# Query and key preparation re-timed, and a bias row copied by another engine, in a fused attention and gated-MLP kernel

## The chip, the core and the metric

The kernel runs on one core of a Trainium2 chip. The core has five engines that run side by side, each in the order of its own instruction list: TensorE (PE, matrix products), VectorE (DVE), ScalarE (ACT), GpSimd (POOL) and SyncE (SP, here only a queue that issues transfers). Transfers run on 16 DMA engines. The metric is the device time of one execution in microseconds (us). The kernel before has a median of 343.76 us over 13 runs (342.1 to 346.02).

## The reference

Attention with normalised queries and keys is followed by a gated MLP with a spatial mix over the sequence. There are 8 batches, 12 heads, a sequence of 448 and a head size of 64; the model width is 768 and the hidden width 1024.

```python
def rmsnorm(x, g):
    rms = np.sqrt(np.mean(x * x, axis=-1, keepdims=True) + 1e-06)
    return x / rms * g
q_n, k_n = (rmsnorm(q, g_q), rmsnorm(k, g_k))
scores = scale * np.matmul(q_n, k_n.transpose(0, 1, 3, 2))
scores = scores - np.max(scores, axis=-1, keepdims=True)
attn = np.exp(scores)
attn = attn / (np.sum(attn, axis=-1, keepdims=True) + 1e-09)
attn_out = np.matmul(attn, v)
# x: attn_out with the heads of a token side by side, (8, 448, 768)
h = np.maximum(x @ w_in, 0.0)
u, v = (h[..., :d_ff // 2].copy(), h[..., d_ff // 2:].copy())
v_n = (v - mu) / np.sqrt(var + 1e-06)
v_s = np.einsum('ts,bsd->btd', w_spatial, v_n) + b_spatial[None, :, None]
gated = u * v_s
return gated @ w_out
```

## The kernel before

**Groups and steps.** Four heads of one batch form a group G; there are 24 groups, three to a batch (b = G // 3). The keys of two heads at a time are split into 7 chunks, so all the work on scores is 168 passes p (group p // 7, chunk p % 7). Two passes make a step s, so a group takes three and a half steps. Passes 0 to 19 are done one at a time in the early part (`early(p)`); steps 10 to 83 form the main loop. In each step TensorE computes scores (line 367, and line 363 for the mixed chunk), ScalarE takes their exponential (`expo`, line 374), and the rest of TensorE's time is filled from a list of MLP pieces (`work`, `fill`), except in a step in which a group is finished (`attend`: weights times v, line 396, with the reciprocal on ScalarE, lines 403 and 404, and the product on VectorE, line 411). The order is written out by hand: the program's order of calls is each engine's order of instructions. After step 83 only the rest of the last batch's MLP remains.

**Preparing q and k.** Before a group's scores can start, six things are done for q (i = 0) and k (i = 1): loading; `squares` on GpSimd (line 250; a few on ScalarE, line 248); `reduce` on VectorE (line 258); `rstd` on ScalarE (lines 266 and 267, for q and k at once); `scaled` (line 277, on GpSimd except for a few early ones); a transpose. The first four groups are transposed by TensorE, all others by a DMA transpose that SP issues (`transpose_dma`, line 341); q is then ready as qT, while k lands as kr and VectorE multiplies it by the combined gains (`k_scale`, line 347, writing kT). The main loop takes these actions out of `todo`, which holds for each step what is to be done for which group. EVEN and ODD give the steps as offsets from 7 * (G // 2), the step in which an even group's scores begin; an odd one's begin in the middle of the step at offset 3. `at` puts a transpose one step after its `scaled`.

**Loads.** Groups 1 to 5 are loaded one by one (`load`, four DMAs for q and four for k, three rotating buffers each). From batch 2 on, q and k of a whole batch are loaded in four parts each (`load_part`, line 105), into two buffers that alternate by batch; the second buffer exists from step 17, when the early buffers are given up. `load_v` loads and converts v of a batch in four parts, issued on GpSimd's queue (line 130), into one of two tiles, also alternating. The weights come over GpSimd's queue as well: `load_w_in` (line 199, one half of w_in each), `load_w_sp` (lines 204 and 205) and `load_w_out` (line 209).

**The spatial weights.** In the MLP of batch 0, after the matmuls of u, `bias_row` writes the spatial bias into a row of the transposed spatial weights w_spT, and `w_sp_unit` transposes w_spatial on TensorE (line 218) and copies it out on VectorE (line 223). bias_row is three VectorE copies of one partition:

```python
dve.tensor_copy(out=main[:, :, 0:64],
                in_=b[:, 0:256].rearrange("o (r m) -> o m r", m=4)[:, 0:3, :])
dve.tensor_copy(out=main[:, :, 64:128], in_=b[:, 256:S].rearrange("o (r m) -> o m r", m=3))
dve.tensor_copy(out=row[:, 384:S], in_=b[:, 3:256:4])
```

Of the kernel before, what the change touches and what calls it, by code (L numbers as in the profile page):

```python
# [10 lines left out]
FP = mybir.dt.float32  # L11
BF = mybir.dt.bfloat16
AF = mybir.ActivationFunctionType
# [6 lines left out]
def kernel(  # L20
# [76 lines left out]
    def load_part(b, i, part):  # L97
        if part == 0:
            t = qb_pools[b % 2].tile([P, 2 * NG, NCH, D], FP, name="kb" if i else "qb")
            qbs[b, i] = t  # L100
            for g in range(NG):
                raw[NG * b + g, i] = t.rearrange("p (h g) c d -> p h g c d", g=NG)[:, :, g]
        lo, hi = lo_hi((q, k)[i][b])
        tv = qbs[b, i].rearrange("p h c d -> p h (c d)")
        sync.dma_start(
            out=(tv[0:64, :, 0:256], tv[64:128, :, 0:192], tv[64:128, :, 192:448], tv[0:64, :, 256:448])[part],
            in_=(lo[:, 0:6], hi[:, 0:6], lo[:, 6:12], hi[:, 6:12])[part])
# [30 lines left out]
    load_first(1, 1, sync)  # L138
# [12 lines left out]
    load(1, 1, pool)  # L151
# [73 lines left out]
    def bias_row():  # L225
        row = w_spT[64:65, NT - 1, :]
        b = bst[64:65, :]
        main = row[:, 0:384].rearrange("o (m r) -> o m r", r=P)
        dve.tensor_copy(out=main[:, :, 0:64],
                        in_=b[:, 0:256].rearrange("o (r m) -> o m r", m=4)[:, 0:3, :])  # L230
        dve.tensor_copy(out=main[:, :, 64:128], in_=b[:, 256:S].rearrange("o (r m) -> o m r", m=3))
        dve.tensor_copy(out=row[:, 384:S], in_=b[:, 3:256:4])
# [353 lines left out]
    squares(0, 1, 0)  # L586
    reduce(0, 0, 0)
# [23 lines left out]
    def early(p):  # L611
        if p == 0:
            squares(1, 0, eng=act)
            squares(1, 1)
            load_v(0, range(4))
            transpose_first(0, 1, dve)
            transpose_first(1, 1, dve)
        elif p == 2:
            reduce(1, 0)
            reduce(1, 1)  # L620
        elif p == 3:
            rstd(1)
            scaled(1, 0, eng=dve)
            scaled(1, 1, eng=dve)
            squares(2, 0)
            squares(2, 1)
            load_w_in(1)
        elif p == 7:
            reduce(2, 0)
            reduce(2, 1)  # L630
        elif p == 8:
            rstd(2)
            scaled(2, 1)
            scaled(2, 0, eng=dve)
            squares(3, 0)
            squares(3, 1)
            load_w_in(0)
        elif p in (9, 10, 11):
            attend(0, (p - 10,))
        elif p == 14:  # L640
            reduce(3, 0)
            reduce(3, 1)
        elif p == 15:
            rstd(3)
            scaled(3, 1)
            scaled(3, 0, eng=dve)
            squares(4, 0)
            squares(4, 1)
            load_w_sp()
        elif p in (16, 17, 18):  # L650
            attend(1, (p - 17,))
        if p not in (0, 6, 9, 10, 11, 13, 16, 17, 18):
            dummies(6)

    pass_scores(0)
    for p in range(2 * S0):
        expo(psp[p], p, 1)
        if p in (6, 13):
            transpose_pe(p // NCH + 1, 0, dve)
            transpose_pe(p // NCH + 1, 1, dve)  # L660
        if p in (4, 5):
            load(4, p - 4)
        if p in (10, 11):
            load(5, p - 10)
        if p + 1 < 2 * S0:
            pass_scores(p + 1)
        early(p)
# [3 lines left out]
    EVEN = {-8: ("sq", 0), -7: ("sq", 1), -6: ("red",), -5: ("rstd",), -4: ("sc", 0), -3: ("sc", 1), -1: ("ks",)}  # L671
    ODD = {-6: ("sq", 0), -5: ("sq", 1), -4: ("red",), -3: ("rstd",), -2: ("sc", 0), -1: ("sc", 1), 2: ("ks",)}
    todo = {}

    def at(s, G, *what):
        todo.setdefault(s, []).append((G,) + what)
        if what[0] == "sc":
            at(s + 1, G, "tr", what[1])

    at(10, 4, "red")  # L680
    at(11, 4, "rstd")
    at(11, 4, "sc", 0)
    at(11, 4, "sc", 1)
    at(13, 4, "ks")
    at(11, 5, "sq", 0)
    at(12, 5, "sq", 1)
    at(13, 5, "red")
    at(14, 5, "rstd")
    at(14, 5, "sc", 0)
    at(14, 5, "sc", 1)  # L690
    at(16, 5, "ks")
    for G in range(6, NGT):
        for o, what in (ODD if G % 2 else EVEN).items():
            at(7 * (G // 2) + o, G, *what)
    for b in range(2, B):
        s0 = max(S0 if b == 2 else 17, NCH * NG * b // 2 - 17)
        for n in range(8):
            at(s0 + n // (2 if b < 4 else 1), NG * b, "ld", n)

    def prep(s, early_act):  # L700
        for G, what, *i in todo.get(s, ()):
            if (what == "rstd") != early_act:
                continue
            if what == "ld":
                load_part(G // NG, *divmod(i[0], 4))
            elif what == "sq":
                squares(G, i[0])
            elif what == "red":
                reduce(G, 0)
                reduce(G, 1)  # L710
            elif what == "rstd":
                rstd(G)
            elif what == "sc":
                scaled(G, i[0])
            elif what == "tr":
                transpose_dma(G, i[0])
# [7 lines left out]
    v_step = {10 + i: (1, [i]) for i in range(4)}  # L724
# [10 lines left out]
    for s in range(S0, NST):  # L735
        if s == 17:
# [68 lines left out]
```

## Time and profile before

| | value |
|---|---|
| median of 13 runs | 343.76 us (342.1 to 346.02) |
| the profiled execution's own time | 342.37 us |
| its span, first to last instruction | 340.6 us |
| granted TensorE clock, mean | 0.952 |
| step 10 begins its exponential at | 40.80 us |
| step 24 | 105.99 us |
| step 75 | 282.23 us |
| step 83, the last | 309.29 us |
| HBM read and written | 38.55 MB and 11.01 MB |

The profile is one execution. A step is found in it by counting: the exponentials over 128x1792 numbers are those of steps 10, 11, 12 and so on to 83. "Idle before" is the time that an engine stood still ahead of an instruction, with what ended the wait. A busy time of TensorE contains overlap between matmuls that follow each other; what it lost is read from its waits. The share of the DMA engines in a window adds up transfers that overlap, so it can exceed 1.

### The profile page before, as it was taken

The page shows a single profiled execution, that of the slowest core. Times are in us where ns is not written, and L with a number is a line of the kernel's source. Part 1 is how long each engine was busy: PE and PEld are TensorE (multiplying, and loading weights), DVE is VectorE, ACT ScalarE, POOL GpSimd, SP SyncE. Part 2 cuts the span into 40 slices and gives each one's busy share as a digit, 9 for nine tenths or more (in the row PEclk, how much of TensorE's full clock was granted, in tenths as well). Part 3 has the DMA queues.
Part 4 walks back from the last instruction along what each step waited for, and adds up shares of the span by engine and source line. Part 5 has one row for each costly group of instructions (what it writes and reads, how often), then busy time and mean ns, then how long its engine had stood idle before and what let it go on. Part 6 is the DMA issues. An engine that isn't in the chain of part 4 may idle for free.

```text
span 340.6 us, 6451 instructions
## 1 busy us (share of the span) xinstructions
PE 274.7 (81%) x2527; PEld 128.2 (38%) x2537; DVE 212.4 (62%) x343; ACT 211.3 (62%) x273; POOL 205.3 (60%) x183
## 2 busy tenths in 40 slices
PE   6577693690498889788788889779699979999994
PEld 6344330240243344334334344334344433444552
DVE  3885615499939467487467484495397486645652
ACT  2687781392067868567477778658477786675421
POOL 6758893789408499529908698359735993020210
PEclk9799997796589999999999999999799999999998
DMA  6999999939991999936993999857957288131145
GB/s 168 190 213 220 209 176 198 165 48 164 152 163 27 172 185 282 195 64 114 239 213 63 190 190 253 174 102 115 261 120 122 45 172 125 24 93 48 24 139 164
DMA packets 82944, 50.90 MB, mean 149 GB/s; under 512 B 46753, under 2 KB 79170, under 8 KB 82914
## 3 DMA queue, kind: packets, MB, share of 16 engines
q1 hardware_dynamic: 67218, 41.53, 61.7%
q0 software_dynamic: 15408, 8.73, 20.4%
q8 instruction: 20, 0.33, 0.5%
q10 hardware_dynamic: 288, 0.23, 0.2%
q14 instruction: 10, 0.08, 0.1%
HBM read 38.55 MB, written 11.01 MB: 146 GB/s over the span
## 4 chain that ended last, share of the span: by engine, by line
PE 25%; POOL 20%; DMA 18%; DVE 17%; issue 9%; ACT 7%; SPq 4%; POOLq 0%; DVEq 0%; ACTq 0%
DMA kr<-n 9%; POOL sqt L250 8%; POOL n L277 6%; DVE ms L258 6%; PE ps L396 5%; PE ps L527 4%; PE ps L508 4%; ACT et L374 4%; DMA kf<-in_k_dram 4%; PE ps L468 4%; PE ps L498 4%; PE pss L367 3%; DMA vt<-in_v_dram 3%; DVE s L476 3%; POOL vn L490 2%
## 5 line engine op out<-in xcount | busy, mean ns | idle before, releaser
L374 ACT ACTIVATE et<-pss 128x1792 bf16<-128x1792 f32 x74 | 122.8, 1660 | 63.9 <-PE pss L367 53.2
L411 DVE TENSOR_TENSOR xt<-ps,rc 128x448 bf16<-128x448 f32 x48 | 28.1, 620 | 60.0 <-ACT rc L404 47.0
L367 PE MATMUL pss<-qT,kT 64*128 64x448 bf16 x254 | 38.4, 362 | 25.8 <-DVE kT L347 21.4
L250 POOL TENSOR_TENSOR sqt<-kb 128x896 f32<-128x896 f32 x18 | 30.3, 1683 | 46.2 <-DVE ms L258 23.5
L527 PE MATMUL ps<-w_out,gt 128*128 128x384 bf16 (+1 forms) x256 | 47.6, 328 | 3.0 <-DVE osb L445 2.2
L396 PE MATMUL ps<-et,vt 128*32 128x448 bf16 x768 | 44.8, 368 | 5.9 <-DMA vt<-in_v_dram 3.7
L258 DVE TENSOR_REDUCE ms<-sqt 128x14 f32<-128x896 f32 x46 | 47.7, 1075 | 2.6 <-POOL sqt L250 2.6
L468 PE MATMUL ps<-w_in_v,xt 128*128 128x512 bf16 (+1 forms) x182 | 45.4, 381 | 0.4
L498 PE MATMUL ps<-xt,w_in_u 128*128 128x448 bf16 x192 | 40.4, 353 | 2.6 <-DVE osb L445 1.9
L347 DVE TENSOR_SCALAR_CACHE_REDUCE kT<-kr,g_col 128x896 bf16<-128x896 bf16 x20 | 22.7, 1135 | 30.7 <-DMA kr<-n 30.7
L367 PEld LDWEIGHTS <-kT 64*128 64x128 bf16 x276 | 10.5, 94 | 59.8 <-issue 30.5
L527 PEld LDWEIGHTS <-gt 128*128 128x128 bf16 (+1 forms) x256 | 24.2, 100 | 22.6 <-issue 9.3
L396 PEld LDWEIGHTS <-vt 128*32 128x32 bf16 x768 | 22.1, 100 | 24.3 <-issue 11.7
L486 POOL TENSOR_SCALAR nm<-mv 128x4 f32<-128x4 f32 x8 | 1.8, 221 | 48.8 <-DVE mv L477 48.8
L277 POOL TENSOR_TENSOR n<-qb,rs 128x896 bf16<-128x896 f32 x18 | 30.4, 1689 | 0.7 <-ACT rs L267 0.7
L277 POOL TENSOR_TENSOR n<-kb,rs 128x896 bf16<-128x896 f32 x18 | 30.4, 1689 | 0.1
L250 POOL TENSOR_TENSOR sqt<-qb 128x896 f32<-128x896 f32 x18 | 30.3, 1681 | 0.0
L445 DVE COPY osb<-ps 128x384 f32<-128x384 f32 (+1 forms) x45 | 24.4, 556 | 9.3 <-PE ps L527 6.9
L508 PE MATMUL ps<-w_spT,vn 128*128 128x448 bf16 (+1 forms) x128 | 28.7, 369 | 0.0
L490 POOL TENSOR_SCALAR vn<-vs,nm,rv 128x512 bf16<-128x512 bf16 (+1 forms) x32 | 24.0, 764 | 7.1 <-ACT rv L485 6.3
L498 PEld LDWEIGHTS <-w_in_u 128*128 128x128 bf16 x192 | 17.3, 97 | 21.9 <-issue 8.4
L468 PEld LDWEIGHTS <-xt 128*128 128x128 bf16 (+1 forms) x192 | 17.7, 100 | 19.9 <-issue 5.7
(94 smaller groups left out, 363.7 us busy)
## 6 DMA issues: line engine op xcount, KB each, us to landing
out_dram<-osb SPq DMA_DIRECT2D x55, 192.0 KB, 3.8
qb<-in_q_dram SPq DMA_DIRECT2D x12, 384.0 KB, 6.1
kb<-in_k_dram SPq DMA_DIRECT2D x12, 384.0 KB, 6.9
qb<-in_q_dram SPq DMA_DIRECT2D x12, 288.0 KB, 5.5
kb<-in_k_dram SPq DMA_DIRECT2D x12, 288.0 KB, 6.7
vt<-in_v_dram POOLq DMA_DIRECT2D x16, 192.0 KB, 5.2
vt<-in_v_dram POOLq DMA_DIRECT2D x16, 144.0 KB, 5.2
qf<-in_q_dram SPq DMA_DIRECT2D x10, 128.0 KB, 4.1
```

The costliest lines, as they stand in the source:

```text
L250: pool.tensor_tensor(out=t, in0=x, in1=x, op=ALU.mult)
L258: dve.tensor_reduce(out=sqs[gk][:, key[1], :], in_=sqt.pop(key).rearrange("p h c d -> p (h c) d"), axis=AX.X, op=ALU.add)
L277: (eng or pool).tensor_tensor(out=t.rearrange("p c h d -> p h c d"), in0=raw[key], in1=rst[gk][:, key[1], :].rearrange("p (h c) -> p h c", ...
L367: pe.matmul(out=ps[:, h, 0:S], lhsT=kT[r, c0:c0 + 128], rhs=qT[r, :], start=True, stop=True, tile_position=(64 * h, 0))
L374: act.activation(out=ets[s][:, 2 * a:2 * a + 2 * m, :], in_=ps[:, 0:2 * m, 0:S], func=AF.Exp, bias=0.0, scale=1.0)
L396: pe.matmul(out=ps[32 * l:32 * l + 32, 0:S], lhsT=w, rhs=et_of(G, 3 if r == 3 else r + 4 * y, h), start=(r == 0), stop=(r == 3), tile_posi ...
L411: dve.tensor_tensor(out=xts[b][:, 2 * g + half, :], in0=pst.pop((G, half))[:, 0:S], in1=rec[G], op=ALU.mult)
L468: pe.matmul(out=ps[0:m, :], lhsT=xts[b][:, j, t0:t0 + m], rhs=w_in_v[:, j, :], start=(j == 0), stop=(j == 5), tile_position=(0, 0))
L490: pool.tensor_scalar(out=vn_t[b % 2][0:m, c, :], in0=vs[b][c][0:m, :], scalar1=nms[b][0:m, c:c + 1], scalar2=rvs[b][0:m, c:c + 1], op0=ALU ...
L498: pe.matmul(out=ps[:, 0:S], lhsT=w_in_u[:, j, 128 * f:128 * f + 128], rhs=xts[b][:, j, :], start=(j == 0), stop=(j == 5))
L508: pe.matmul(out=ps[:, 0:S], lhsT=vn_t[b % 2][0:kp, c, 128 * f:128 * f + 128], rhs=w_spT[0:kp, c, :], start=(c == 0), stop=(c == NT - 1))
L527: pe.matmul(out=ps[o:o + m, 0:384], lhsT=gts[b][f][:, t0:t0 + m], rhs=w_out[:, f, r], start=(f == 0), stop=(f == 3), tile_position=(0, o))
```

## The change

- `bias_row`: the three copies are made by ScalarE instead of VectorE.
- Start: the second k load of group 0 is issued from ScalarE's queue instead of SP's; the k load of group 1 on GpSimd's queue comes after the first square on that engine; some early squares move between GpSimd and ScalarE; w_in's two halves come earlier on GpSimd's queue.
- v of batch 1 is loaded in pass 9 of the early part, ahead of the spatial weights of pass 15; before, its four parts came in steps 10 to 13.
- Batch 2 (groups 6, 7 and 8) is loaded group by group with `load`. From batch 3 on the whole-batch loads stay, and the second buffer is opened at step 24. They are grouped more tightly: q's four parts in two steps, and k's in two (odd batch) or four (even batch).
- EVEN and ODD become tables that give q and k steps of their own. Squares never fall two in a step in the steady part; `scaled` comes at -6 and -5 (before -4 and -3) for an even group and at -3 and -2 (before -2 and -1) for an odd one. The transposes come at -5 and -4 (before -3 and -2) and at -2 and -1 (before -1 and 0); `k_scale` stays at -1 and 2. Groups 4 to 8 have tables of their own. Inside a step the actions are sorted by ORDER.

```diff
@@ load_part, start
-            t = qb_pools[b % 2].tile([P, 2 * NG, NCH, D], FP, name="kb" if i else "qb")
+            t = qb_pools[(b + 1) % 2].tile([P, 2 * NG, NCH, D], FP, name="kb" if i else "qb")
...
-    load_first(1, 1, sync)
+    load_first(1, 1, act)
...
-    load(1, 1, pool)
@@ bias_row
-        dve.tensor_copy(out=main[:, :, 0:64],
-                        in_=b[:, 0:256].rearrange("o (r m) -> o m r", m=4)[:, 0:3, :])
-        dve.tensor_copy(out=main[:, :, 64:128], in_=b[:, 256:S].rearrange("o (r m) -> o m r", m=3))
-        dve.tensor_copy(out=row[:, 384:S], in_=b[:, 3:256:4])
+        for o, i in ((main[:, :, 0:64], b[:, 0:256].rearrange("o (r m) -> o m r", m=4)[:, 0:3, :]),
+                     (main[:, :, 64:128], b[:, 256:S].rearrange("o (r m) -> o m r", m=3)),
+                     (row[:, 384:S], b[:, 3:256:4])):
+            act.activation(out=o, in_=i, func=AF.Copy, bias=0.0, scale=1.0)
@@ early
     squares(0, 1, 0)
+    load(1, 1, pool)
...
         if p == 0:
-            squares(1, 0, eng=act)
             squares(1, 1)
             load_v(0, range(4))
+            load_w_in(1)
+            squares(2, 1)
+            load_w_in(0)
...
+        elif p == 1:
+            squares(1, 0, eng=act)
...
-            squares(2, 0)
-            squares(2, 1)
-            load_w_in(1)
+        elif p == 4:
+            squares(2, 0, eng=act)
...
-        elif p == 8:
+        elif p == 9:
             rstd(2)
+            scaled(2, 0, eng=dve)
             scaled(2, 1)
-            scaled(2, 0, eng=dve)
             squares(3, 0)
             squares(3, 1)
-            load_w_in(0)
-        elif p in (9, 10, 11):
-            attend(0, (p - 10,))
+            load_v(1, range(4))
...
+        elif p == 19:
+            reduce(4, 0)
+        if p in (10, 11, 12):
+            attend(0, (p - 11,))
...
+        if p in (16, 17):
+            load(6, p - 16)
@@ main loop
-    EVEN = {-8: ("sq", 0), -7: ("sq", 1), -6: ("red",), -5: ("rstd",), -4: ("sc", 0), -3: ("sc", 1), -1: ("ks",)}
-    ODD = {-6: ("sq", 0), -5: ("sq", 1), -4: ("red",), -3: ("rstd",), -2: ("sc", 0), -1: ("sc", 1), 2: ("ks",)}
+    EVEN = {"sq": (-11, -8), "red": (-9, -7), "rstd": (-6,), "sc": (-6, -5), "tr": (-5, -4), "ks": (-1,)}
+    ODD = {"sq": (-9, -7), "red": (-6, -5), "rstd": (-3,), "sc": (-3, -2), "tr": (-2, -1), "ks": (2,)}
+    FIRST = {4: {"red": (None, 10), "rstd": (11,), "sc": (11, 11), "tr": (11, 11), "ks": (13,)},
+             5: {"sq": (10, 11), "red": (11, 12), "rstd": (13,), "sc": (13, 14), "tr": (14, 14), "ks": (16,)},
+             6: {"sq": (13, 14), "red": (14, 15), "rstd": (16,), "sc": (16, 17), "tr": (17, 17), "ks": (20,)},
+             7: {"ldg": (12, 12), "sq": (15, 17), "red": (17, 18), "rstd": (19,), "sc": (19, 19), "tr": (19, 20),
+                 "ks": (23,)},
+             8: {"ldg": (15, 15), "sq": (18, 20)}}
...
-    for b in range(2, B):
-        s0 = max(S0 if b == 2 else 17, NCH * NG * b // 2 - 17)
-        for n in range(8):
-            at(s0 + n // (2 if b < 4 else 1), NG * b, "ld", n)
+    SC8 = 23
+    for b in range(3, B):
+        first_q = max(15 if b == 3 else SC8 + 1, (21 * b - 38) // 2)
+        for n in range(4):
+            todo.setdefault(first_q + n // 2, []).append(("ld", NG * b, n))
+            todo.setdefault(first_q + 2 + (n if b % 2 == 0 else n // 2), []).append(("ld", NG * b, n + 4))
+
+    ORDER = ("red", "rstd", "sc", "sq", "tr", "ks", "ldg", "ld")
...
-    v_step = {10 + i: (1, [i]) for i in range(4)}
+    v_step = {}
...
-        if s == 17:
+        if s == SC8 + 1:
             early_sb.close()
```

## The prediction

> **What bounds the kernel now.** I read the page's busy shares, then TensorE's waits, then the places where its long waits stand. The lines are from the page (three), the waits (four), the timeline around 74 to 90 us (six), the timeline around 160 to 169 us (three) and the windows (three).
>
> ```profile
> PE 274.7 (81%) x2527; PEld 128.2 (38%) x2537; DVE 212.4 (62%) x343; ACT 211.3 (62%) x273; POOL 205.3 (60%) x183
> ...
> PE   6577693690498889788788889779699979999994
> ...
> DMA  6999999939991999936993999857957288131145
> ...
> PE pss L367 <- DVE kT L347: 21.4, 10, 5.0
> PE ps L218 <- DVE w_spT L223: 12.5, 1, 12.5
> PE ps L396 <- DMA vt<-in_v_dram: 3.7, 1, 3.7
> ...
> DVE kT L347 <- DMA kr<-n: 30.7, 9, 7.8
> ...
> 74.11 13.55 DVE L229 CAST w_spT<-bst 1x192 bf16<-1x192 f32 x1
> 74.63 1.68 POOL L277 TENSOR_TENSOR n<-qb,rs 128x896 bf16<-128x896 f32 x1
> ...
> 87.41 1.72 POOL L250 TENSOR_TENSOR sqt<-qb 128x896 f32<-128x896 f32 x1
> 87.58 1.72 DVE L231 CAST w_spT<-bst 1x192 bf16<-1x192 f32 x1
> 89.22 0.19 DVE L232 CAST w_spT<-bst 1x64 bf16<-1x64 f32 x1
> ...
> 89.89 2.05 PE L218 MATMUL ps<-ident,w_sp 128*64 128x128 bf16 x20 [12.54 <-DVE w_spT L223]
> ...
> 161.31 1.31 SPq L341 DMA_TRANSPOSE kr<-n  x1
> ...
> 167.61 1.15 DVE L347 TENSOR_SCALAR_CACHE_REDUCE kT<-kr,g_col 128x896 bf16<-128x896 bf16 x1 [3.80 <-DMA kr<-n]
> ...
> 168.82 0.55 PE L367 MATMUL pss<-qT,kT 64*128 64x448 bf16 x4 [2.47 <-DVE kT L347]
> ...
> 0.00:60.00 60.00, 40.43 (x453) 22.80 (x454) 34.23 (x60) 36.75 (x54) 43.31 (x46) 0.94 1.10 197
> 60.00:110.00 50.00, 33.10 (x279) 14.17 (x282) 39.03 (x44) 24.67 (x33) 31.44 (x26) 0.80 0.88 120
> 110.00:250.00 140.00, 118.93 (x1111) 52.61 (x1115) 85.65 (x146) 96.33 (x118) 96.76 (x81) 0.99 0.94 177
> ```
>
> To be seen: TensorE is the busiest engine, and its strip is at 9 only towards the end; it has a hole at about 77 to 90 us. The second and third wait lines are one event each. The first is ten events, all of one kind: a group's scores stand ready to start, but its kT isn't there. One of the ten, of 5.0 us, is group 4 at 55.98 us; the other nine (16.4 us) lie after 120 us, once in a step that begins a group. The timeline of group 12 shows why: its kr was issued at 161.31, landed 6.3 us later, and VectorE and then TensorE waited for it. The last number of a window line is GB/s, the one before it the share of the DMA engines, the one before that the clock: up to 60 us the transfers run flat out at 197 GB/s; from 60 to 110 us, with the hole in it, only at 120.
>
> The hole has an odd cause. Three bias copies of one partition, 192, 192 and 64 numbers, took 13.55, 1.72 and 0.19 us. Size can't be it, since the first two are equal. From 74.63 to 89.13 us GpSimd ran without a pause, and the copies ended with it.
>
> **What the Trainium skill says.** "SBUF — State Buffer", section "Who interferes with whom": VectorE and GpSimd share a pair of ports under an exclusive lock; a VectorE copy or cast from SBUF to SBUF can enter a two-port mode, and then waits for GpSimd's instruction (or GpSimd for it); "PE and ACT never wait on anyone." The trace agrees so far as the 13.55 us beside a busy GpSimd go. It shows no ScalarE copy of this shape. "DMA: Bandwidth & Descriptors", section "Queues, rings and completion order": each DMA engine takes turns between the queues that have work for it, packet by packet. So a GpSimd load that comes sooner takes time from SP's loads and transposes, and the bytes ahead of a transpose count whichever queue they are in. The trace agrees with this: kr of group 4, issued at 46.70 in the flat-out stretch, landed after 7.9 us, those of quiet stretches after 2.9.
>
> **The change part by part**, against the profiled execution: 342.37 us, of which the span is 340.6.
>
> (a) Bias row on ScalarE. The wait of 12.54 us goes. The clock line helps: it is granted 0.50 at 80 to 90 us and 0.69 at 90 to 100 us, and step 20 takes 3.98 us where neighbours take 3.0; I count 1.0 us for that. Added: three ScalarE instructions. Nearest rows: 0.30 us for 128x4, 0.52 for 128x384; so some 0.35 each, 1.0 in all, in a step in which ScalarE has about half a microsecond idle: 0.5 us on the path. If ScalarE had to wait for the lock as well, the wait would only move; the skill's sentence excludes it, and I take its word. What is late next: steps 20 to 24 need groups 6 and 7. Their kr were issued at 79.1 and 93.9, so with the hole gone the transposes have to come sooner too. Before, VectorE's own list (squares' sums behind the copy) and SP's were held up by the hole; they move with it. Sum: -13.0.
>
> (b) v of batch 1 in pass 9. Before, the last part was issued on GpSimd's queue at 52.61 and landed 10 us later, which held TensorE 3.73 us. Pass 9 comes at about 27 us and its queue there is free of squares by some 31, so v lands by 45, ten microseconds before use: -3.7. Its DMA time isn't new, only earlier.
>
> (c) Group 4's kT (5.00 us). The transposes are issued in step 11 right after the scaling, as before in effect (qT at 44.7, 0.06 us after its scaling). What delays kr is DMA. By SBUF bytes, ahead of it lie groups 0 to 5 (12 x 0.46 MB), batch 2's q (1.38), v of batches 0 (0.69) and 1 (a quarter), w_in (1.57) and w_sp (0.40): 9.7 MB, and 9.7 MB at 197 GB/s is 49 us. After: group 6 alone in place of batch 2's q (0.92), but all of v 1: 9.8 MB. So it is about as late. The gain is between 0 and 5.0; I take 2.0, since nothing of GpSimd's queue competes any more while it travels.
>
> (d) The nine later waits, 16.4 us. Groups 8, 10, 12, 14, 16 and 18 (even) make 12.4 of them, and in each VectorE waited for kr (1.2 to 4.4 us). Their transposes move two steps, about 6 us, sooner at 3.0 us a step: all six should go. Group 13 (0.95, kr landed late) moves one step: goes. Groups 11 and 17 (1.54 and 1.53) had kr landed 10 us before; there VectorE was late with its own list, where the multiplication keeps its place behind the statistics of the MLP: they stay. Together 13.3; but loads are denser (four parts in two steps, up to 1.38 MB in 6 us, 230 GB/s against the 177 of the window) and a kr may fall behind them, so I take -12.0. Bounds: -4 to -16.4.
>
> (e) The early part, up to step 10. The first k square comes before k of group 1 is fetched, so that fetch starts at about 8.4 instead of 2.7 us and its square ends near 16.7; the sums of pass 2 were done after 17 us anyway. The pass gets one more square on ScalarE (0.94 us), which is loaded there: +0.5. GpSimd's queue takes DMA share earlier (w_in's second half at about 23 instead of 31 us), so groups 3 and 4 land later, perhaps 2 us; against it SP's loads start two issues (1.3 us) sooner. Bounds -1.5 to +3; taken +0.5.
>
> (f) Whole-batch loads, and single-group loads for batch 2: 16 more DMAs on SP at 0.6 us, 10 us of SP's time. SP waited 72.6 us for GpSimd's scaling alone, so this costs nothing; without that cover it would delay transposes, which is the first rival.
>
> Sum: -13.0 - 3.7 - 2.0 - 12.0 + 0.5 = -30.2, or 312.2 us for the profiled execution. That one lies 0.4% under the median of 343.76, so the forecast is 313 us. A test against bytes: to begin step 24, at 105.99 before, the loads of batches 0 to 3, w_in, w_sp and the transposes up to group 7, some 17 MB, must be through; at 197 GB/s that is 86 us. My parts (a) to (c) and (e) put step 24 at 88. So there is hardly any room left there, and the DMA engines are the next bound up to step 24.
>
> **Rivals.** *The transfers take over* (0.23): the hole goes, but the DMA engines, flat out up to 90 us and then in denser bursts, bring kr late, so that of (c) nothing and of (d) only 4 us come, and the early part loses 2: 342.4 - 13.0 - 3.7 - 4 + 2 = 323.7, in the median 325. For it: share 1.10 and 0.94. Against: four or five steps of notice for kr where there were two or three. *Everything goes* (0.08): all of (c) and (d) and nothing early: 342.4 - 13.0 - 3.7 - 5 - 16.4 = 304.3, median 305. *The copy isn't cured* (0.03): ScalarE needs as long on single-partition rows; only (b) to (e) come, about 329. Against it: 1.72 us for equal work. *Slower* (0.06): kr behind the bursts. Each of the 19 groups after the fourth has about 9 us (three steps) from kr's issue to its multiplication; median landing is 5.6, the longest seen 12.1. To lose the 17 us of (a) and (b) and the 16.4 that are there now, every group would have to wait 1.8 us, which takes a landing of 11 us in the median, twice the present one: then 344 or more.
>
> **How the numbers follow.** The main case has 0.60, with its own range of 308 to 318. The range for 8 in 10 takes in most of the second case and the third: 304 to 327. Half a per cent, about 1.7 us, is what a measurement of this kernel tells from no change. Faster by more: 0.60 + 0.23 + 0.08 + 0.03 = 0.94; the last case gives 0.01 to no change and 0.05 to slower.
>
> **What would show it.** (a) right: no w_spT wait over 1 us, and the ScalarE copies under 1 us each. (b): no wait of line 396 for v. (c): group 4's wait at 3 us. (d): the wait of scores for kT falls from 21.4 to about 7, with two of 1.5 us left. (e): step 10 between 39 and 44 us. (f) and the first rival: kr landing in the median above 8 us, and VectorE waiting for kr over 20 us. Wrong altogether if step 24 begins after 95 us, or if steps 24 to 75 take more than 172 of their 176.2.

## The result, and the profile after

The changed kernel takes 317.67 us in the median of 11 runs (312.48 to 322.59), against 343.8 us for the kernel before in the runs beside it. The ratio is 0.919, with a 95% interval of 0.9145 to 0.9228: some 8% faster, 26 us between the medians. The ratio compares only the executions within 1.5% of the fastest of each kernel, so it lies a little below 317.67 / 343.8 = 0.924, and the profiled execution after, at 319.19 us, isn't among these while that before is. The forecast of 313 us was 4.7 us too low, and 317.67 lies in its range of 304 to 327. The profiled execution has a span of 317.3 us, 23.3 us shorter than that of the profile before. Line numbers after are smaller by one than before (scores L366, kT L346, bias copies L231).

The first three lines are of the page of the changed kernel (busy shares, the strips of TensorE and of the transfers); the next two are of its waits.

```profile
PE 276.7 (87%) x2527; PEld 128.7 (41%) x2537; DVE 197.4 (62%) x340; ACT 212.1 (67%) x277; POOL 203.6 (64%) x182
...
PE   7558759997298999879999899979999999999994
...
DMA  5899995889995999999979999998735592132156
```

```profile
PE pss L366 <- DVE kT L346: 11.9, 5, 5.7
...
DVE kT L346 <- DMA kr<-n: 10.9, 3, 8.3
```

TensorE's busy share rises from 81% to 87% for the same number of matmuls. The hole, an empty slice and one at "4" behind it, is gone, but one slice at "2" has come at about 79 to 87 us. The waits for w_spT and for v are no longer in the list; the waits for kT have fallen from 21.4 to 11.9 us, and the largest of them is a new one, of 5.7 us.

Here is that place in the timeline of the changed kernel (start, duration, engine, line, what it does, idle time before it and what ended it):

```profile
66.20 2.61 SPq L105 DMA_DIRECT2D qb<-in_q_dram  x4
...
67.37 1.11 ACT L231 ACTIVATE w_spT<-bst 1x192 bf16<-1x192 f32 x3
...
68.98 3.67 SPq L340 DMA_TRANSPOSE qT<-n  x1
...
72.76 3.27 SPq L340 DMA_TRANSPOSE kr<-n  x1
...
84.54 1.15 DVE L346 TENSOR_SCALAR_CACHE_REDUCE kT<-kr,g_col 128x896 bf16<-128x896 bf16 x1 [8.31 <-DMA kr<-n]
...
85.75 0.93 PE L366 MATMUL pss<-qT,kT 64*128 64x448 bf16 x4 [5.74 <-DVE kT L346]
```

The three bias copies take 1.11 us together on ScalarE. But kr of group 6, issued at 72.76 us, lands only at 84.5, 11.8 us later; VectorE stands 8.31 us for it and TensorE 5.74 us.

The windows of the changed kernel, in the stretches used before (the last three numbers are clock, share of the DMA engines and GB/s):

```profile
0.00:60.00 60.00, 44.53 (x490) 24.97 (x492) 36.41 (x62) 38.64 (x56) 44.07 (x47) 0.89 0.94 190
60.00:110.00 50.00, 40.86 (x337) 17.09 (x342) 28.63 (x50) 32.19 (x43) 37.99 (x33) 0.86 1.10 172
110.00:250.00 140.00, 129.50 (x1209) 57.09 (x1206) 95.64 (x162) 104.95 (x132) 107.91 (x90) 0.99 1.01 174
```

From 60 to 110 us the transfers now carry 172 GB/s instead of 120, at a share of 1.10 instead of 0.88: the slack that they had in the old hole has gone.

Where the 23.3 us came from follows from the starts of the steps' exponentials in the two profiles:

| stretch | before, us | after, us | difference |
|---|---|---|---|
| start to step 10 | 40.8 | 45.1 | +4.3 |
| steps 10 to 14 (group 4's kT) | 17.6 | 12.0 | -5.6 |
| steps 14 to 16 (v of batch 1) | 10.5 | 5.6 | -5.0 |
| steps 16 to 20 (bias row, w_spT) | 24.4 | 13.6 | -10.8 |
| steps 20 to 24 (groups 6 and 7) | 12.7 | 22.2 | +9.5 |
| steps 24 to 75 | 176.2 | 160.7 | -15.6 |
| step 75 to the end | 58.3 | 58.2 | -0.1 |

Differences are of unrounded starts. Each column is one execution. Steps 16 to 20 and 20 to 24 belong together: what the first gain, the second give back but for 1.3 us. So the question for the experiments: was the hole of 12.5 us worth anything by itself?

### The profile page after: what moved, and what is told of

Its sections match the earlier page's. It is cut to its first block, busy times and chain, and to the rows that moved or that the text cites. A ratio compares the mean times of both kernels' runs of the same rounds, so it can differ in the third digit from the quotient of the medians.

```text
span 317.3 us, 6478 instructions
## 1 busy us (share of the span) xinstructions
PE 276.7 (87%) x2527; PEld 128.7 (41%) x2537; DVE 197.4 (62%) x340; ACT 212.1 (67%) x277; POOL 203.6 (64%) x182
## 4 chain that ended last, share of the span: by engine, by line
PE 37%; DMA 17%; POOL 13%; DVE 11%; ACT 9%; SPq 7%; issue 4%; ACTq 0%; POOLq 0%; DVEq 0%
PE ps L526 9%; DMA kf<-in_k_dram 8%; PE ps L467 7%; PE ps L507 6%; ACT et L373 6%; PE pss L366 6%; POOL sqt L249 5%; PE ps L395 5%; DMA kb<-in_k_dram 5%; POOL n L276 4%; PE ps L497 4%; DVE ms L257 3%; POOL vn L489 3%; DMA kr<-n 2%; DVE s L475 2%
## 5 line engine op out<-in xcount | busy, mean ns | idle before, releaser
L257 DVE TENSOR_REDUCE ms<-sqt 128x14 f32<-128x896 f32 x46 | 49.3, 1076 | 19.2 <-POOL sqt L249 18.6
L366 PE MATMUL pss<-qT,kT 64*128 64x448 bf16 x254 | 39.2, 366 | 18.0 <-DVE kT L346 11.9
L526 PE MATMUL ps<-w_out,gt 128*128 128x384 bf16 (+1 forms) x256 | 48.8, 332 | 1.2 <-ACT rs L266 0.5
L395 PE MATMUL ps<-et,vt 128*32 128x448 bf16 x768 | 43.0, 361 | 1.7 <-ACT lr L402 1.7
L276 POOL TENSOR_TENSOR n<-qb,rs 128x896 bf16<-128x896 f32 x15 | 25.4, 1693 | 25.1 <-ACT rs L266 25.0
L249 POOL TENSOR_TENSOR sqt<-kb 128x896 f32<-128x896 f32 x15 | 25.1, 1682 | 11.1 <-DMA kb<-in_k_dram 11.1
L366 PEld LDWEIGHTS <-kT 64*128 64x128 bf16 x276 | 10.8, 94 | 51.7 <-issue 30.9
L346 DVE TENSOR_SCALAR_CACHE_REDUCE kT<-kr,g_col 128x896 bf16<-128x896 bf16 x20 | 22.7, 1136 | 11.0 <-DMA kr<-n 10.9
L395 PEld LDWEIGHTS <-vt 128*32 128x32 bf16 x768 | 21.0, 100 | 19.4 <-issue 5.6
L497 PEld LDWEIGHTS <-w_in_u 128*128 128x128 bf16 x192 | 17.4, 98 | 21.3 <-issue 7.7
L276 POOL TENSOR_TENSOR n<-kb,rs 128x896 bf16<-128x896 f32 x15 | 25.4, 1693 | 0.1
L249 POOL TENSOR_TENSOR sqt<-qb 128x896 f32<-128x896 f32 x15 | 25.2, 1679 | 0.0
```

Of the source, the lines that this page charges most:

```text
L249: pool.tensor_tensor(out=t, in0=x, in1=x, op=ALU.mult)
L257: dve.tensor_reduce(out=sqs[gk][:, key[1], :], in_=sqt.pop(key).rearrange("p h c d -> p (h c) d"), axis=AX.X, op=ALU.add)
L276: (eng or pool).tensor_tensor(out=t.rearrange("p c h d -> p h c d"), in0=raw[key], in1=rst[gk][:, key[1], :].rearrange("p (h c) -> p h c", ...
L366: pe.matmul(out=ps[:, h, 0:S], lhsT=kT[r, c0:c0 + 128], rhs=qT[r, :], start=True, stop=True, tile_position=(64 * h, 0))
L395: pe.matmul(out=ps[32 * l:32 * l + 32, 0:S], lhsT=w, rhs=et_of(G, 3 if r == 3 else r + 4 * y, h), start=(r == 0), stop=(r == 3), tile_posi ...
L497: pe.matmul(out=ps[:, 0:S], lhsT=w_in_u[:, j, 128 * f:128 * f + 128], rhs=xts[b][:, j, :], start=(j == 0), stop=(j == 5))
```

## Experiments

The kernel before ran beside each. A ratio is to it, with its 95% interval.

**1. The bias row on ScalarE, and nothing else.** Edit to the kernel before:

```diff
-        dve.tensor_copy(out=main[:, :, 0:64], in_=...)
-        dve.tensor_copy(out=main[:, :, 64:128], in_=...)
-        dve.tensor_copy(out=row[:, 384:S], in_=...)
+        for o, i in (...the same three...):
+            act.activation(out=o, in_=i, func=AF.Copy, bias=0.0, scale=1.0)
```

> The kernel before with only its three bias copies made by ScalarE. My theory (the hole of 12.5 us is the whole price, and the rest moves up with it): 13 us faster than before, about 331, w_spT waits under 1 us, no new wait of scores for kT of more than 2 us. The rival (the transfers were idle in the hole and have to do the same bytes anyway, so part of the hole comes back as a later kr for groups 6 and 7): 5 to 9 us faster, about 336, with a wait for kT of 3 us or more between 70 and 95 us.

Measured: 344.03 us, ratio 1.0007 (0.9967 to 1.0048): no gain at all. The theory fails, and the rival is right in kind only: not a part of the hole comes back, but nearly the whole. The timeline of this kernel shows it.

```profile
74.40 1.12 ACT L232 ACTIVATE w_spT<-bst 1x192 bf16<-1x192 f32 x3
...
79.72 1.65 SPq L341 DMA_TRANSPOSE kr<-n  x1
...
83.38 11.61 SPq L341 DMA_TRANSPOSE qT<-n  x1
...
93.65 1.15 DVE L347 TENSOR_SCALAR_CACHE_REDUCE kT<-kr,g_col 128x896 bf16<-128x896 bf16 x1 [12.80 <-DMA kr<-n]
...
94.86 0.93 PE L367 MATMUL pss<-qT,kT 64*128 64x448 bf16 x4 [11.92 <-DVE kT L347]
```

The copies take 1.12 us together and the wait for w_spT is gone: step 20 begins at 81.0 instead of 93.3 us. Then TensorE stands 11.92 us for kT of group 6, and step 22 begins at 100.0, before at 100.3. kr of group 6 was issued at 79.72; in the kernel before it was issued at 79.1 and landed at 91.2. The hole began at 77.35 us (89.89 less the wait of 12.54), and kr of group 6 was issued 1.7 us later, right after its scaling on GpSimd (77.01 to 78.71): the hole had not held the transpose up. It lay over a second wait of nearly the same length, and hid it.

**2. The bias row back on VectorE in the changed kernel.** The edit is that of experiment 1 reversed.

> The changed kernel with the three bias copies back on VectorE. If the lock of the shared ports is the cause, the copies take as long as GpSimd runs without a pause there, several us or more, and the time is 5 to 13 us over the changed kernel's 317.7. If the re-timed preparation leaves GpSimd pauses enough (the rival), the copies are through in under 3 us and the time is within 2 us of the changed kernel.

Measured: 316.25 us, ratio 0.9207 (0.9137 to 0.9277), not to be told from the changed kernel's 0.9187. The timeline of this kernel:

```profile
67.44 0.38 DVE L228 CAST w_spT<-bst 1x192 bf16<-1x192 f32 x1
67.75 6.47 DVE L230 CAST w_spT<-bst 1x192 bf16<-1x192 f32 x1
74.14 0.19 DVE L231 CAST w_spT<-bst 1x64 bf16<-1x64 f32 x1
...
68.33 1.68 POOL L276 TENSOR_TENSOR n<-kf,rs 128x896 bf16<-128x896 f32 x1
69.98 1.67 POOL L249 TENSOR_TENSOR sqt<-kf 128x896 f32<-128x896 f32 x1
71.61 0.73 POOL L130 DMA_DIRECT2D vt<-in_v_dram  x1
72.35 1.69 POOL L249 TENSOR_TENSOR sqt<-qf 128x896 f32<-128x896 f32 x1
```

One copy stands 6.47 us beside a busy GpSimd, as the theory has it, and TensorE waits 4.08 us for w_spT. Yet the theory's loss of time doesn't come. The wait for w_spT takes the place of the wait for kT of group 6, which falls from 5.74 to 0.13 us; kr of group 6 is again late, 9.3 us after its issue. Then TensorE waits 3.97 us for kT of group 7, and step 24 begins at 95.7 us.

**3. Is it the lock?** In the kernel before, the three copies stay on VectorE but as multiplications by one that also write their sum.

```diff
-        dve.tensor_copy(out=..., in_=...)
+            dve.tensor_scalar(out=o, in0=i, scalar1=one_c[64:65, :], scalar2=None, op0=ALU.mult,
+                              op1=ALU.add, accum_out=tot_b[64:65, :])
```

> The kernel before with the bias copies still on VectorE and in the same places, but as a multiply by 1 that also writes its sum, the form in which k is multiplied in this kernel. If the cause is the wait for ports shared with GpSimd, which the skill says this form doesn't use, each takes under 0.5 us and the time is that of the bias copies on ScalarE alone, within 2 us. If the cause is the shape (one partition, strided numbers) or VectorE's list, the first still takes over 5 us and the time stays within 2 us of before, 344.

The timeline of this kernel has the copies at 0.56, 0.48 and 0.32 us:

```profile
74.55 0.56 DVE L235 TENSOR_SCALAR_CACHE_REDUCE w_spT<-bst,one_c 1x192 bf16<-1x192 f32 x1
...
75.15 0.48 DVE L235 TENSOR_SCALAR_CACHE_REDUCE w_spT<-bst,one_c 1x192 bf16<-1x192 f32 x1
...
75.67 0.32 DVE L235 TENSOR_SCALAR_CACHE_REDUCE w_spT<-bst,one_c 1x64 bf16<-1x64 f32 x1
...
72.11 3.02 POOL L494 TENSOR_SCALAR vn<-vs,nm,rv 128x512 bf16<-128x512 bf16 x4 [2.20 <-ACT rv L489]
75.11 1.68 POOL L281 TENSOR_TENSOR n<-qb,rs 128x896 bf16<-128x896 f32 x1
```

GpSimd is busy beside them, from 72.11 to 76.79 us. So VectorE itself wasn't late, nor were its operands: the form of the instruction decided. The Trainium skill says this ("SBUF — State Buffer", "Who interferes with whom": the scalar form that also writes its accumulator doesn't take the shared pair), and this run agrees. The whole took 340.94 us, ratio 0.989 (0.9805 to 0.9976): 3.1 us under the median of experiment 1 where at most 2 us apart were expected, and a gain of about 1% over the kernel before. What makes this small difference was not found. Again TensorE then waited for kT of group 6, 11.54 us: the second way to cure the copy leaves the same second wait.

**4. The transposes late again.** In the changed kernel, scaling and transposes have the offsets of the kernel before; the whole-batch loads from batch 4 on are one or two steps later with them, and the second buffer opens at step 26 instead of 24.

```diff
-    EVEN = {... "rstd": (-6,), "sc": (-6, -5), "tr": (-5, -4), ...}
-    ODD = {... "sc": (-3, -2), "tr": (-2, -1), ...}
+    EVEN = {... "rstd": (-5,), "sc": (-4, -3), "tr": (-3, -2), ...}
+    ODD = {... "sc": (-2, -1), "tr": (-1, 0), ...}
...
-    SC8 = 23
+    SC8 = 25
...
-        first_q = max(15 if b == 3 else SC8 + 1, (21 * b - 38) // 2)
+        first_q = max(15 if b == 3 else SC8 + 1, (21 * b - 38) // 2 + (1 if b % 2 else 2))
```

> The changed kernel with scaling and transposes of the groups from 8 on put back to the steps of before (even -4 and -3, odd -2 and -1, the transposes one step after each); squares and sums stay as changed, and the whole-batch loads follow one or two steps later, since they wait for the scaling. My theory (the earlier transposes make the gain after step 24): waits for kT return, to 20 us or more in all, and the time goes up by 9 to 14 us, to about 329. The rival (spread squares and denser loads make it): within 3 us of the changed kernel.

Measured: 326.55 us, ratio 0.9504 (0.943 to 0.9579): 8.9 us over the changed kernel by the medians, 10.9 by the ratios, about as the theory has it. The waits for kT come to 14.1 us in all, though, not to 20 or more. The profiled execution took 328.65 us, 2.1 over the median. In it steps 24 to 75 take 172.4 us instead of 160.7. TensorE's waits in those steps, first of this kernel, then of the changed one (total, times, longest):

```profile
PE pss L366 <- DVE kT L346: 9.7, 7, 2.8
PE ps L526 <- DVE xt L410: 4.4, 3, 1.9
```

```profile
PE pss L366 <- DVE kT L346: 6.2, 4, 1.9
...
PE ps L526 <- DVE xt L410: 0.2, 1, 0.2
```

Both kT lines contain one wait for group 7, of 1.94 and 1.25 us, that ends just ahead of step 24; without it they are 7.7 and 4.9. So of the 11.7 us that these steps lose, 2.8 are waits for kT and 4.2 waits for VectorE, named by its product xt. Most of the rest shows as TensorE's busy time, 155.9 against 150.1 us for about the same matmuls, at a granted clock of 0.96 against 0.99. How much of that belongs to the edit and how much to the single execution isn't shown: over whole executions of the changed kernel the granted clock goes from 0.939 to 0.971. The later loads are part of the edit too. Still, the loss in the medians is about three times the lost waits for kT.

**5 to 7. Is w_out what delays kr of group 6?** w_out (768 KB) was issued at 79.98 us in experiment 1, just behind kr. It was loaded three or four steps sooner in three kernels: experiment 1 with that edit (5), the kernel before with it alone (6), the changed kernel with it (7).

```diff
-        if s == 18:
+        if s == 15:
             load_w_out()
```

(In 7 the step is 14.)

> The kernel before with the bias copies on ScalarE (as in the run of that alone, 344.0, which gained nothing because scores then waited 11.9 us for group 6's kT, its kr landing 13.9 us after its issue), and w_out loaded in step 15 instead of 18, where the transfers are nearly idle. Theory: the long w_out transfer, in flight together with kr of groups 6 and 7, is the second hole that lies beside the first; then the wait for group 6 falls under 3 us and the time to 331 to 335. Rival: the many loads of batch 3 hold kr up, w_out doesn't matter: wait of 8 us or more, time 340 to 345.

> The kernel before with w_out loaded in step 15, and nothing else. If there are two holes side by side, the bias copies' hole stays and hides the gain: 341 to 344, with the w_spT wait of over 10 us still there. If the hole at 77 to 90 us was made by the transfers alone and the copy's length is a symptom, the copy gets short and the time falls to 331 to 335.

> The changed kernel with w_out loaded in step 14 instead of 18. Theory (w_out beside kr of group 6): steps 20 and 21, 15.4 us before, take 8 or less, and the time is 5 to 8 us under the changed kernel's 317.7. Rival (batch 3's loads and v of batch 2 hold kr up whatever w_out does): within 2 us of it.

Measured: (5) 339.48 us, ratio 0.9859 (0.9751 to 0.9966); (6) 341.4 us, ratio 0.9954 (0.9924 to 0.9984); (7) 315.61 us, ratio 0.912 (0.8993 to 0.9248). In (5) kr of group 6, issued at 77.39, lands after 8.9 us instead of 13.9, and TensorE's wait falls from 11.92 to 6.93 us: w_out was a part of it there, less than the theory has it and more than the rival. In (6) kr lands after 9.8 us instead of 12.1, but the wait for w_spT stays at 11.74 us and hides that, as two waits over each other must. (The profiled execution of (5) took 335.38 us, 4.1 under the median.) In (7) nothing moves: the timeline of that kernel has kr landing 11.0 us after issue with w_out issued 13 us ahead of it.

```profile
60.76 0.84 POOL L208 DMA_DIRECT2D w_out<-in_moe_w_out_dram  x1
...
74.20 3.47 SPq L340 DMA_TRANSPOSE kr<-n  x1
...
85.20 1.15 DVE L346 TENSOR_SCALAR_CACHE_REDUCE kT<-kr,g_col 128x896 bf16<-128x896 bf16 x1 [8.50 <-DMA kr<-n]
```

So in the changed kernel something else holds kr.

**8. k of group 1 fetched first again.** In the changed kernel, its load on GpSimd's queue goes back ahead of the first square.

```diff
+    load(1, 1, pool)
     eps = const.tile([P, 1], FP)
...
     squares(0, 1, 0)
-    load(1, 1, pool)
```

> The changed kernel with k of group 1 fetched where it was before, ahead of the first square on GpSimd's queue. Theory (that late fetch makes the square of k in group 1 late, and with it VectorE's sums, ScalarE's passes 3 to 6 and all of the early part): step 10 comes at 42 us or sooner instead of 45.1 in the changed kernel's profile, and the time falls by 2 to 3 us. Rival (w_in's earlier place, or the squares put on ScalarE, make the early part long): step 10 within 1 us of the changed kernel's.

Measured: 317.33 us, ratio 0.9202 (0.9076 to 0.9328). The square of that k begins at 9.70 instead of 15.56 us, and step 10 at 42.96; in six other profiles with the changed early part it begins at 43.4 to 45.1. The lead of 1 or 2 us can't be seen in the time: inconclusive.

**9. Batch 3 behind the transposes.** In the changed kernel, the loads of q and k of batch 3 begin in step 17. Within a step transposes go first, so those of group 6 stand ahead of these bytes on SP's queue.

```diff
-        first_q = max(15 if b == 3 else SC8 + 1, (21 * b - 38) // 2)
+        first_q = max(17 if b == 3 else SC8 + 1, (21 * b - 38) // 2)
```

> The changed kernel with the whole-batch loads of batch 3 begun in step 17 instead of 15. Inside a step the transposes are issued ahead of loads, so kr of group 6 now stands ahead of all of batch 3's bytes (1.34 MB of q were ahead of it on SP's queue). Theory: what holds kr of group 6 for 11.8 us is the bytes in front of it on its own queue. Then it lands 3 to 6 us after issue, TensorE's wait of 5.7 us for kT of group 6 falls under 2 us and step 22 begins at about 87 instead of 91.6; the whole gains 1 to 5 us over 317.7, since group 9's squares (step 19) may then wait for their q. Rival, the bytes of v of batch 2 and w_out on GpSimd's queue hold it: kr of group 6 still lands 9 us or more after issue and the wait stays at 4 to 6 us, within 2 us of 317.7.

The timelines of this kernel: SP and what follows on the other engines.

```profile
66.37 1.25 SPq L340 DMA_TRANSPOSE qT<-n  x1
...
70.25 1.22 SPq L340 DMA_TRANSPOSE kr<-n  x1
...
71.52 3.57 SPq L105 DMA_DIRECT2D qb<-in_q_dram  x4
...
84.51 1.68 POOL L249 TENSOR_TENSOR sqt<-qb 128x896 f32<-128x896 f32 x1 [5.48 <-DMA qb<-in_q_dram]
...
88.58 1.08 DVE L257 TENSOR_REDUCE ms<-sqt 128x14 f32<-128x896 f32 x1 [9.00 <-POOL sqt L249]
...
90.25 0.58 PE L467 MATMUL ps<-w_in_v,xt 128*128 128x512 bf16 x1 [5.40 <-DVE xt L410]
```

The mechanism is right: kr of group 6 lands 4.3 us after issue, where it took 9.3 to 11.8 us in all eight other profiles with the changed loads of batches 2 and 3. VectorE doesn't wait for it, and TensorE's wait for group 6 is gone. What the changed kernel's kr stood behind was the load of q of batch 3 (1.38 MB), issued just ahead of it on SP's queue. The Trainium skill says that each DMA engine consumes the descriptors of one ring in order, without a promise that they finish in order ("DMA: Bandwidth & Descriptors", "Queues, rings and completion order"); this run agrees with the first. No run put these bytes on another queue, so whether the queue counts, or only the bytes issued earlier, isn't shown. The price was wrong: 322.66 us, ratio 0.9446 (0.9387 to 0.9505), 5 us slower than the changed kernel by the medians and 8.9 by the ratios. q of batch 3 is late now: GpSimd's square waits for it, VectorE's sum 9.00 us for the square, xt stands behind the sum, and TensorE waits 5.40 us for xt. A wait of 3.91 us for kT of group 7 follows. Step 24 begins at 100.7 us, in the changed kernel at 98.4, and at 93.3 to 97.4 in the other seven profiles.

**10. v of batch 2 later, in steps 20 to 23.** In the changed kernel, which issues it in steps 16 to 19:

```diff
-            v_step.update({s + 4 + i: (b + 2, [i]) for i in range(4)})
+            v_step.update({s + (8 if b == 0 else 4) + i: (b + 2, [i]) for i in range(4)})
```

> The changed kernel with v of batch 2 loaded in steps 20 to 23 instead of 16 to 19; SP's queue is as in the changed kernel. Theory (SP's own queue holds kr of group 6): no help, kr lands 9 us or more after issue, the wait for kT of group 6 stays at 4 to 6 us; v may then be late for step 25 (a wait of up to 4 us); 315 to 322. Rival, GpSimd's queue holds it: two of four v parts and most of their 0.67 MB leave the window, kr of group 6 lands within 6 us of issue, the wait falls under 2 us and step 22 begins at about 88; 312 to 316.

Measured: 317.35 us, ratio 0.9296 (0.9228 to 0.9364). kr of group 6 lands after 9.7 us, TensorE waits 2.25 us for it, and step 22 begins at 88.0. The landing and the time are as the theory has it, step 22 is as the rival has it, and the wait lies between them. But kernels that leave v of batch 2 alone come to much the same: kr lands after 10.0 us in experiments 11 and 12, and step 22 begins at 87.9 in experiment 11. So a part of GpSimd's bytes of v in the delay isn't shown.

**11. w_in in passes 3 and 9, as before.** In the changed kernel:

```diff
-            load_w_in(1)
             squares(2, 1)
-            load_w_in(0)
...
             scaled(1, 1, eng=dve)
+            load_w_in(1)
         elif p == 4:
...
             squares(3, 1)
+            load_w_in(0)
             load_v(1, range(4))
```

> The changed kernel with the two halves of w_in back in passes 3 and 9 (the changed kernel issues both in pass 0). Step 10 begins at 42.96 to 45.05 us in five profiles with the changed early part and at 40.4 to 41.2 in five with the old one. Theory: 1.57 MB of w_in ahead of groups 2 and 3 take the transfers' time from the first loads, and that is the loss; then step 10 comes back to 41 to 42.5 and the whole gains 1 to 3 us. Rival, the loss is in the order of squares and sums on ScalarE and VectorE (the late first k square, the square in pass 4): step 10 stays at 43 to 45 and the whole within 1.5 us of 317.7.

Measured: 317.3 us, ratio 0.9282 (0.9213 to 0.9351), step 10 at 44.3 us. The rival's numbers came: the earlier weights aren't what the early part loses, as far as one profile shows.

**12. The whole early part as before.** The start and passes 0 to 18 of the kernel before, with v of batch 1 in pass 8, and everything from step 10 on as changed.

```diff
-    load_first(1, 1, act)
+    load_first(1, 1, sync)
...
+    load(1, 1, pool)
     eps = const.tile([P, 1], FP)
...
-            squares(1, 1)
+            squares(1, 0, eng=act)
+            squares(1, 1)
...
-        elif p == 4:
-            squares(2, 0, eng=act)
+            squares(2, 0)
+            squares(2, 1)
+            load_w_in(1)
...
-        if p in (10, 11, 12):
-            attend(0, (p - 11,))
+        elif p in (9, 10, 11):
+            attend(0, (p - 10,))
```

> The changed kernel with the early part (start and passes 0 to 18) of the kernel before: old issue order of the first loads, k of group 1 ahead of the first GpSimd square, old order of squares and sums, w_in in passes 3 and 9, attention of group 0 in passes 9 to 11. v of batch 1 is loaded in pass 8 behind w_in, and all from step 10 on is as changed. Theory (e): the early part's new order loses 3 to 4 us, so step 10 begins at 40.4 to 41.5 instead of 43 to 45, and the following steps keep that lead: 312 to 315.5. Rival, step 24 is set by the bytes that must have come by then, so a lead at step 10 is lost again by step 24 (95 to 99 us, as in the changed kernel), group 6 or group 7 waits longer: 316 to 319.

Measured: 316.22 us, ratio 0.9202 (0.9173 to 0.9231), not to be told from the changed kernel. Step 10 begins at 42.0 us, in the changed kernel at 45.1. In the profile the lead is 5.1 us at step 24 (93.3) and 2.9 at step 75, because steps 24 to 75 take 162.9 instead of 160.7 us. The two profiled executions differ more than the medians, and other profiles with the new early part have step 24 at 94.3 us too (experiments 8 and 10), so neither theory is shown.

No version here is measurably faster than the changed kernel; experiment 7 has the lowest median, 315.61 us, within its scatter.

## Why the prediction held, and where it didn't

The time fell into the range, and the sum was 7 us too good: 312.2 us for the profiled execution, which took 319.19. One large term, (a), fell short by 11.7 us, and (b) and (d) together came out 4.8 us better than taken. That the errors cancelled so far is luck, and the range, which also held the 325 us of the first rival, could not tell the two accounts apart. By its own signs the prediction was half wrong. Step 24 began at 98.4 us, where anything after 95 was to mean "wrong altogether", and step 10 at 45.05, outside 39 to 44. The waits for kT fell to 11.9 us, not 7. No wait for w_spT or v was left, kr landed in a median of 5.1 us, and steps 24 to 75 took 160.7 us: these signs spoke for it.

**(a) The bias row: -13.0 forecast, nothing measured alone.** The copies went as priced: 1.1 us for three on ScalarE against 1.0 forecast, and the wait for w_spT vanished. That ScalarE doesn't wait for the shared ports, taken from the skill, held: 0.55, 0.45 and 0.30 us beside a GpSimd that worked from 65.54 to 71.84 us. The step that failed is the one about what is late next: "Before, VectorE's own list (squares' sums behind the copy) and SP's were held up by the hole; they move with it." They don't. Experiment 1 issued kr of group 6 at 79.7 us, as before (79.1), and it landed at 93.6. The profile before had the numbers needed:

```profile
79.06 1.46 SPq L341 DMA_TRANSPOSE kr<-n  x1
...
92.28 1.13 DVE L347 TENSOR_SCALAR_CACHE_REDUCE kT<-kr,g_col 128x896 bf16<-128x896 bf16 x1
...
96.71 0.55 PE L367 MATMUL pss<-qT,kT 64*128 64x448 bf16 x4
```

kr of group 6 landed at 91.2 us and the multiplication takes 1.1, so with that landing group 6 could not begin before about 92.4, hole or no hole. It began at 96.71. Unless kr came sooner, at most 4.3 us of the 12.5 were to be had. In the changed kernel the transposes do come sooner (72.8), and still steps 16 to 24 together gain only 1.3 us of the 13.0.

**(b) v of batch 1: -3.7 forecast.** TensorE's wait for v is gone, and steps 14 to 16 are 5.0 us shorter. That part wasn't tried by itself. The wait was real on the path in the experiments that kept the old place: 5.41 us in experiment 1.

**(c) Group 4's kT: -2.0 taken, the whole wait went.** But it went partly into (e). kr landed at 53.5 us, before at 54.6, about as late as the forecast said. It was issued later, at 50.6 instead of 46.7, because the early part was later, and landed after 2.9 us: from 50 to 60 us the share of the DMA engines is 0.78, before 1.31. So steps 10 to 14 are 5.6 us shorter and step 10 is 4.3 us later; together -1.4, where (c) and (e) together said -1.5. The step that failed is the reason: bytes ahead of it were taken as what sets its landing. Experiment 12 issued it at 47.6 us, and it landed at 51.2, with much the same bytes ahead. What held it in the kernel before stays open.

**(d) The later kT waits: -12.0 forecast, -11.5 measured, and 4 us more beside it.** Of the nine waits of 16.4 us after 120 us, three are left: group 10 with 1.17 us, and groups 11 and 17 with 1.88 and 1.89 us, the two that were forecast to stay. The median landing of kr is 5.1 us (before 5.6), so the first rival's mechanism did not come in this stretch. The stretch gained 15.6 us in all. Most of the other 4 is a wait that the sum didn't have: TensorE's waits for VectorE's copies osb, 5.4 us in steps 24 to 75 before, are not in the list after. Experiment 4 supports the cause, with 8.9 to 10.9 us in the time and 11.7 in these steps, though its loads were moved as well.

**(e) The early part: +0.5 forecast, +4.3 in the profile, 2.6 to 4.3 over six profiles.** The bound of +3 was too low. About half of it is there at pass 7, whose exponential begins at 24.9 us instead of 22.75. The square of group 1's k stood 5.23 us for its late data; with that undone (experiment 8) pass 7 begins at 24.0 and step 10 at 42.96, so it is less than half of this half. The other half comes between pass 7 and step 10, and its cause stays open. w_in is not it (experiment 11). The old early part brings step 10 back to 42.0, not 40.8 (experiment 12). How much of it costs time at the end stays open too: the medians of experiment 12 and of the changed kernel differ by 1.5 us, inside their scatter, and the ratios (0.9202 and 0.9187) the other way.

**(f) More DMAs on SP: 0 forecast.** Wrong at one place. From 60.59 to 68.81 us SP issues loads almost without a pause, eight of group 8 and four of batch 3. q of group 6 had been scaled at 64.5, and its transpose was issued at 68.98, 4.5 us later. In experiment 9, without batch 3's four loads ahead, it was issued at 66.37. The step that failed is "SP waited 72.6 us for GpSimd's scaling alone, so this costs nothing": such cover is a sum over the whole span, and in this stretch there was none.

**The rivals and the byte test.** The first rival was right in kind about steps 20 to 24: with the hole gone, TensorE waited for transfers there. Its number for the time (325) was wrong because (d) came nearly in full. The forecast of step 24 at 88 us failed against 98.4 here, and against at least 93.3 in every other profile with these loads. The transfers moved 181 GB/s on average up to that point, not much under the 197 assumed, and 197 was no ceiling (the kernel before itself moved 221 GB/s from 30 to 40 us); what stood before TensorE was the order of issue on SP, where a transpose that is needed next comes behind 1.38 MB that are needed later. Experiment 9 shows that the other order isn't free either. Which loads could be left out of that stretch without making others late was not found.

**What isn't separated.** About 12 us of the gain lie in steps 10 to 24 (65.2 us before, 53.3 after). No run tried the earlier v of batch 1 or the loads of batch 2 by group alone, so how they share it is read from the waits that are gone, not shown by undoing them.

## What to carry to other kernels

Before a long wait is priced at its whole length, look up when the next inputs of the same engine land: a hole is worth only what is left until the next wait, and the profile before showed it here (4.3 of 12.5 us, with kr landing at 91.2). A transpose that is needed soon was late when it was issued behind bulk loads on the same queue, but pushing the loads back makes their consumers late in turn; where a stretch is full of transfers, count what must come by when in queue order, not only in bytes. Outside such a stretch, two steps more of notice for a landing was the best shown part of this change (8.9 to 10.9 us in the time, with the loads that moved along). The waits for VectorE's xt, 4.4 us with late transposes against 0.2, suggest that a late landing also delays what stands behind the waiting instruction.

## What the runs showed of the hardware

- A DMA transpose that takes long to issue on SP also lands late. In all the profiles here, 51 transposes of known landing took 3 us or more to issue (11.61 us at most, in experiment 1), and they landed 6.3 to 17.4 us after the start of issue. A short issue says nothing: kr of group 6 in experiment 1 was issued in 1.65 us and landed after 13.9, and others with 1.2 us landed after 2.9.
- Two equal VectorE copies of 192 numbers took 0.38 and 6.47 us (experiment 2), and before 13.55 and 1.72: a copy can stand for several GpSimd instructions in a row, not for one only, and which of two equal copies stands isn't fixed. The form that also writes its sum took 0.56 and 0.48 us.
- A high share of the DMA engines isn't a high rate. These are windows of the changed kernel:

```profile
30.00:40.00 10.00, 7.49 (x106) 3.74 (x105) 5.45 (x7) 7.99 (x13) 8.77 (x8) 1.00 1.21 239
...
80.00:90.00 10.00, 4.26 (x45) 1.63 (x48) 3.30 (x6) 3.15 (x5) 2.99 (x3) 0.67 1.48 192
```

With the transposes of groups 6 and 7 among the loads, a share of 1.48 carried 192 GB/s; without any transpose, 1.21 carried 239. No run here separates the transposes from what else differs between the two windows.
